# Second batch's pixels loaded uncast and added in rows on GpSimd, keys made two chunks at a time, and 17 instead of 14 GELU chunks on VectorE

## The chip, the cores and the metric

The kernel runs on one core of a Trainium2 chip. The metric is the device time of one execution in microseconds. Before the change it is 950.85 us (median of three runs, 950.6 to 951.17). The profile shown below is of one execution with a span of 949.0 us and a granted TensorE clock of 1.0.

## The reference

An attention over keys that are pooled from an image is followed by a feed-forward layer. Cut to what matters:

```
q: (4, 12288, 128)   kv: (4, 384, 32, 128)   w_sr: (128, 128)
w_in: (128, 2048)    w_out: (2048, 128)

kv_pool = mean over 4 x 4 pixels of kv            # (4, 96, 8, 128): 768 rows per batch
k = v   = kv_pool.reshape(4, 768, 128) @ w_sr
a       = softmax(q @ k^T / sqrt(128))
x       = (a @ v).reshape(49152, 128)
h       = x @ w_in
out     = (h * sigmoid(1.702 * h)) @ w_out        # float32
```

## The kernel before, in words

**Tiling.** The 49152 tokens are cut into 96 groups of 512 (`NG`), 24 per batch. The 768 keys of a batch are six chunks of 128 (`JC`), the 2048 hidden columns are sixteen chunks of 128 (`FCH`). The work goes in two rounds (`R`): attention of groups 0 to 47 (batches 0 and 1), then the feed-forward layer ("MoE") of these groups, then the same for groups 48 to 95. The outputs of attention of one round lie in the SBUF tile `x`, 12 slots of 2048 columns.

**Fill, activation, drain.** A fill multiplies into up to three PSUM banks (L340 for attention, L586 for MoE), one ScalarE activation takes the two or three banks at once (exponential at L342, GELU at L588) and writes into the ring `ag`, and a drain multiplies `ag` with the values (L353) or with `w_out` (L596). Two sets of three banks alternate, so that ScalarE works on one trio while TensorE fills the next. Banks 2, 5, 6 and 7 are for everything else (`acc`), later 6 and 7 alone. VectorE empties them: it divides the attention outputs (L376, L379), and transposes the MoE outputs into `o_sb` (L607), which SyncE stores.

**Chunks that ScalarE is spared.** Some exponentials and, in the second round, 14 GELU chunks (`lent`, one in every third group from 52 to 91) are computed by VectorE in short steps (`early_exp`, `lent_gelu`, L443 to L465) into the tile `aside`.

**The order.** The order of all instructions is written by the kernel itself: a planner at the end of the kernel walks over the fills, keeps a model of when TensorE, the banks and VectorE are free (`COST`, `COPY`, `RECIPROCAL`, in units of one 512-column matmul), and puts drains and extra jobs (`extras`) between the fills. Each engine works off its own queue in that order. `background(i)` is called when the first chunk of group `i` is about to be filled, and starts the loads, casts and stores that hang on this group.

**Keys of the second batch.** The first batch's pixels are loaded at the start. Those of batch 1 follow in `background(10)` and `background(12)`, three chunks each, by `load_chunk` (L130): GpSimd issues a DMA that casts from float32 to bf16, 128 partitions of 2048 columns. `pool_chunk` (L139 to L142) then sums on TensorE: sixteen matmuls with the 128 x 32 matrix `sum4`, four accumulated for each of four column groups, which add four pixels of a row and four rows. `key_and_value` (L161 to L164) multiplies the pooled chunk with `w_sr` for the keys and, transposed, for the values. From group 15 on one chunk's jobs are queued per group. The keys are needed at group 24.

**Queries.** They are cast to bf16 in DRAM by GpSimd's DMAs (`cast_q`, L209, at the groups in `CAST`), and brought back transposed by SyncE (`load_qT`, L215, at the groups in `TURN`). A block is four groups. `gate()` makes GpSimd wait for VectorE's place in the order: VectorE writes one element (L510), then GpSimd writes it (L511), and only then issues what follows.

**Outputs of attention** go to DRAM (`put_away`, L493) and come back transposed (`bring_back`, L499), both on SyncE.

Of the kernel before, what the change touches and what calls it, by code (L numbers as in the profile page):

```python
# [7 lines left out]
F32 = mybir.dt.float32  # L8
F32R = mybir.dt.float32r
I32 = mybir.dt.int32  # L10
BF = mybir.dt.bfloat16
AF = mybir.ActivationFunctionType
AX = mybir.AxisListType
ADD = mybir.AluOpType.add
# [10 lines left out]
def kernel(  # L25
    ctx, tc, q, kv, w_sr, moe_w_in, moe_w_out, out,
):
    nc = tc.nc
    B, N, C = q.shape
    _, H, W, _ = kv.shape  # L30
    r = 4
    Hp, Wp = H // r, W // r
    J = Hp * Wp
    JC = J // 128
    d_ff = moe_w_in.shape[1]
    FCH = d_ff // 128
    scale = 1.0 / (C ** 0.5)
    G = 512
    SG = 4 * G
    NG = B * N // G  # L40
    NS = NG // 4
    GB = NG // B
# [10 lines left out]
    kv_r = kv.rearrange("b (ch p) (a w) c -> b a ch p (w c)", p=128, a=2)  # L53
# [6 lines left out]
    XS = NS // R  # L60
# [7 lines left out]
    kvtmp = ctx.enter_context(tc.tile_pool(name="kvtmp", bufs=1))  # L68
# [3 lines left out]
    opool = ctx.enter_context(tc.tile_pool(name="op", bufs=3))  # L72
# [12 lines left out]
    def acc(key=None):  # L85

        nonlocal last_acc
        last_acc = next_acc()
        turns.append(last_acc)
        turns.remove(last_acc)  # L90
        if key:
            closes[last_acc] = key
        return banks[:, last_acc, :]

    def next_acc():
        return min((m for m in turns if m not in closes), key=lambda m: (max(free[m], now), turns.index(m)))
# [12 lines left out]
    x = xpool.tile([128, XS * SG], BF, name="x")  # L109

    def x_tile(s):
        return x[:, s % XS * SG:(s % XS + 1) * SG]
# [3 lines left out]
    HC = H // 128  # L116
    h = J // 2
    kv_tiles, kv_sums, pooled, pTs, kTs, vs = {}, {}, {}, {}, {}, {}

    def new_keys(b):  # L120
        kTs[b] = kvres.tile([128, J], BF, name="kT")

        vs[b] = kvres.tile([128, JC, C + 8], BF, name="v")
        nc.vector.memset(vs[b][:, :, C:C + 1], 1.0)

    def load_chunk(b, jc):

        a, ch = divmod(jc, HC)
        t = x_tile(XS - 1 - jc)
        nc.gpsimd.dma_start(out=t, in_=kv_r[b, a, ch])  # L130
        kv_tiles[b, jc] = t.rearrange("p (wp w1 c) -> p w1 wp c", w1=r, c=C)

    def pool_chunk(b, jc):
# [7 lines left out]
        pTs[b, jc] = kvtmp.tile([128, 128], BF, name="pTc", bufs=2)  # L141
        nc.vector.tensor_copy(pTs[b, jc], ps[:, 0:128])  # L142

    def key_chunk(b, jc):
        if jc == 0:
            new_keys(b)
        ps = acc()
        nc.tensor.matmul(ps[:, 0:128], w_sr_sb, pTs[b, jc], start=True, stop=True)
        nc.vector.tensor_copy(kTs[b][:, jc * 128:jc * 128 + 128], ps[:, 0:128])
# [5 lines left out]
        vs[b, jc] = True  # L155

    def key_and_value(b, jc):
        if (b, jc) == (1, 0):
            new_keys(b)
        ps = acc()  # L160
        nc.tensor.matmul(ps[:, 0:128], w_sr_sb, pTs[b, jc], start=True, stop=True)  # L161
        nc.tensor.matmul(ps[:, 128:256], pTs.pop((b, jc)), w_sr_sb, start=True, stop=True)
        nc.vector.tensor_copy(kTs[b][:, jc * 128:jc * 128 + 128], ps[:, 0:128])  # L163
        nc.vector.tensor_copy(vs[b][:, jc, 0:C], ps[:, 128:256])  # L164
        vs[b, jc] = True
# [41 lines left out]
    def cast_q(s):  # L207
        sl = slice(s * SG, (s + 1) * SG)
        nc.gpsimd.dma_start(out=q_bf[sl, :].rearrange("(p i) c -> p (i c)", p=128),  # L209
                            in_=q_flat[sl, :].rearrange("(p i) c -> p (i c)", p=128))  # L210

    def load_qT(s):
        qTs[s] = qpool.tile([128, 1, SG], BF, name="qT")
        nc.vector.memset(qTs[s][:, 0, 0:1], 0.0)
        nc.sync.dma_start_transpose(out=qTs[s], in_=q_bf[s * SG:(s + 1) * SG, :])  # L215
# [53 lines left out]
    for m in range(0, 128, 32):  # L269
        p = slice(m, m + 32)  # L270
# [3 lines left out]
    sum4 = cpool.tile([128, 32], BF)  # L274
# [3 lines left out]
    w_sr_sb = cpool.tile([128, C], BF)  # L278
# [40 lines left out]

    early = range(NG // R, NG // R + EARLY)  # L320
    rolling = [(i, JC - 1) for i in [*range(38, NG // R, 6), *range(57, 90, 6)]]
    lent = [(g, FCH - 1) for g in range(52, 94, 3)]
    aside = agpool.tile([128, K, 512], BF, name="aside")

    def weights(c):
# [112 lines left out]
    def lent_gelu(ps, out):  # L438
# [23 lines left out]
        for m in (0, 256):  # L462
            nc.vector.reciprocal(b[:, m:m + 256], a[:, m:m + 256])  # L463
            yield RECIPROCAL
        nc.vector.scalar_tensor_tensor(out, raw, -LN2 / 1.702, b, MUL, MUL)  # L465
# [21 lines left out]
    PART, FIRST = 24, 3  # L487

    def put_away(n, m):
        size = PART // 2 if n == 0 and m > FIRST else PART  # L490
        for o in range(m * PART, m * PART + PART, size):
            lo = n * XS * SG + o * T
            nc.sync.dma_start(out=x_bf[lo:lo + size * T, :].rearrange("(k p) c -> p k c", p=T),  # L493
                              in_=x[:, o * T:(o + size) * T].rearrange("p (k c) -> p k c", k=size))

    def bring_back(n, m):
        o = m * PART
        lo = n * XS * SG + o * T
        nc.sync.dma_start_transpose(out=x[:, o * T:(o + PART) * T].unsqueeze(1), in_=x_bf[lo:lo + PART * T, :])  # L499
# [6 lines left out]
    def gate():  # L506

        one = gate_tile[:, gates[0] % 8:gates[0] % 8 + 1]
        gates[0] += 1
        nc.vector.memset(one, 0.0)  # L510
        nc.gpsimd.memset(one, 0.0)  # L511

    TURN = {6: 3, 7: 4, 8: 5, 20: 6, 21: 7, 22: 8, 30: 9, 32: 10, 35: 11, 40: 12}
    CAST = {0: [5], 13: [6], 14: [7], 15: [8], 25: [9, 10], 26: [11, 12]}
    CAST_MOE = {20: 13, 21: 14, 22: 15, 23: 16, 33: 17, 34: 18, 35: 19, 36: 20, 37: 21, 38: 22, 39: 23}

    def background(i):

        first_round = i < GB * 2
        s = TURN.get(i, NS) if first_round else i // 4 + 3 if i % 4 == 0 else NS  # L520
        if s < NS:
            load_qT(s)
        if i in CAST:
            gate()
            for s in CAST[i]:
                cast_q(s)
        if i in (10, 12):
            gate()
            for jc in range(i % 10 * 3 // 2, i % 10 * 3 // 2 + 3):
                load_chunk(1, jc)  # L530
        if 0 <= i - 16 < JC:
            extras.append((key_and_value, 1, i - 16))
        if 0 <= i - 15 < JC:
            extras.append((pool_chunk, 1, i - 15))
        if i in (28, 33, 38):
            put_away(0, (i - 28) // 5)
        if i in (31, 36, 41):
            bring_back(0, (i - 31) // 5)
        if i == 27:
            gate()  # L540
            nc.gpsimd.dma_start(out=w_in_sb, in_=moe_w_in)
        if i == 28:
            gate()
            nc.gpsimd.dma_start(out=w_out_sb, in_=moe_w_out.rearrange("(o p) c -> p o c", p=128))

# [33 lines left out]
    extras = []  # L579
# [67 lines left out]
    for n in range(R):  # L647
        part = [c for c in chunks if c[0] // (NG // R) == n]
        while part:
            m = sizes.pop(0) if sizes else K  # L650
# [12 lines left out]
        while flat:  # L663
            m = K if len(flat) > sum(rest) else rest.pop(0)
# [25 lines left out]
    def jobs(p):  # L690

        nonlocal now
        for f, *args in first.get(p, ()):
            if f in COST:
                now = max(now, free[next_acc()])
            f(*args)
            if f in COST:
                now += COST[f][0]
                free[last_acc] = copied(f)

    def prepare(p):

        nonlocal now
        kind, part = seq[p]
        for i, jc in part:
            if (kind, i) not in begun:
                begun.add((kind, i))
                (background if kind == "a" else background_moe)(i)
            while kind == "a" and ((key_and_value, i // GB, jc) in extras or (transpose_q, i) in extras):
                f, *args = extras.pop(0)  # L710
                now = max(now, free[next_acc()]) + COST[f][0]
                f(*args)
                free[last_acc] = copied(f)
# [20 lines left out]


    FIXED, CHUNK, SWITCH, HANDOVER, EVACUATE = 0.295, 1.978, 6.0, 1.0, 4.5
    COST = {pool_chunk: (1.9, 2.6), key_chunk: (0.3, 2.4), value_chunk: (0.3, 2.4),
            transpose_q: (1.05, 4.2), early_fill: (1.0, 5.5), key_and_value: (0.55, 3.5),
            transpose_pooled: (0.9, 3.6), make_k: (0.8, 3.2), make_v: (0.8, 3.7)}
    COPY = {pool_chunk: 1.5, key_chunk: 1.5, value_chunk: 1.5, key_and_value: 2.8, transpose_q: 3.2}  # L740
    SMALL = 0.26
    RECIPROCAL = 10.5
    PAUSE = 4.0
    end, extra_at = [], 0.0
    source, dve = None, 0.0
# [2 lines left out]
    def on_dve(cost):  # L748
        nonlocal dve
        dve = max(dve, now + 1.0) + cost  # L750


    def copied(f):
        if f not in COPY:
            return now + COST[f][1]
        on_dve(COPY[f])
        return max(now + COST[f][1], dve)

# [28 lines left out]
    for n in range(len(seq)):  # L787
        fill(n + 2)
        jobs(n + 3)
        while True:  # L790
# [33 lines left out]
            kind, i, c = source[0]  # L824
# [11 lines left out]
            start = now if source is todo_early else max(now, end[needs] + HANDOVER)  # L836
            if first_of:
                start = max(start, bank)
# [44 lines left out]
```

The softmax here doesn't subtract the row's maximum and nothing guards it: scores larger than these inputs give would overflow.

## Time and profile before

| What | Value |
|---|---|
| time, median of 3 | 950.85 us |
| span of the profiled execution | 949.0 us |
| first exponential of ScalarE | 9.2 us |
| first attention phase, first GELU | to 142.3 us |
| first MoE phase | 142.3 to 487.7 us |
| second attention phase | 487.7 to 604.7 us |
| second MoE phase | 604.7 us to the end |
| VectorE busy from 604 to 937 us | 191.6 us of 333 |
| pixels of batch 1: loads issued | 39.0 to 46.4 us |
| pixels of batch 1: time to landing | 7.0 to 12.2 us |
| casts of query blocks 6, 7, 8: issued | 47.4, 49.1, 53.1 us |
| transposes of these blocks: start | 66.0, 68.9, 72.7 us |

How to read it: the page gives the busy time of each engine, the span in 40 slices, the DMA queues, the chain of work that ended last, and the costliest groups of instructions. A group's line names the source line, the engine, the operation, the tile written and read, and the shape; then the busy time, the mean of one in ns, and the idle time just before. A group of matmuls overlaps with itself, so its mean is longer than its pitch. The chain of waits can also be listed in order of time: start, length, and what led. The phases in the table are told apart by ScalarE's table loads [...].

### The profile page before, as it was taken

Reading aid. Unit: us, or ns where it says so; the run is one execution under the profiler, and the core shown is the slowest. Engines: PE = TensorE matmul, PEld = TensorE weight load, DVE = VectorE, ACT = ScalarE, POOL = GpSimd, SP = SyncE. Lnnn points to the kernel's source line nnn. Section 1 sums busy time; section 2 is a strip of 40 time slices with the busy share of each in tenths; the row PEclk is TensorE's granted clock in tenths of the full one; section 3 lists DMA queues with packets and bytes.
Section 4 is the critical chain, followed back from the end, with each engine's and each line's share of the span. In section 5 each row is a group of like instructions: output and inputs, shape, how many; then the busy total and the mean of one; then the engine's idle time right before and its main releaser. Section 6 shows DMA issues by size and latency. Waiting matters only on the chain.

```text
span 949.0 us, 15424 instructions
## 1 busy us (share of the span) xinstructions
PE 941.5 (99%) x6314; PEld 503.1 (53%) x6314; DVE 536.8 (57%) x1037; ACT 933.9 (98%) x708; POOL 67.0 (7%) x115
## 2 busy tenths in 40 slices
PE   8999999999999999999999999999999999999998
PEld 4677776444444444454446777754444444444444
DVE  5643553102477777778655765365666665566631
ACT  5999999999999999999999999999999999999998
POOL 4101001330000232000000000000000000000000
PEclk9999999999999999999999999999999999999999
DMA  9999922999867799865335583552222222222222
GB/s 182 203 181 193 214 57 42 157 127 170 162 132 113 116 147 125 123 103 78 65 55 112 133 160 77 134 122 35 44 34 45 34 46 34 45 33 45 34 45 45
DMA packets 372871, 94.93 MB, mean 100 GB/s; under 512 B 346736, under 2 KB 370416, under 8 KB 372464
## 3 DMA queue, kind: packets, MB, share of 16 engines
q1 hardware_dynamic: 343872, 61.31, 36.5%
q0 software_dynamic: 28656, 32.51, 22.6%
q8 instruction: 49, 0.80, 0.4%
q14 instruction: 22, 0.18, 0.1%
q10 hardware_dynamic: 272, 0.13, 0.0%
HBM read 52.49 MB, written 48.76 MB: 107 GB/s over the span
## 4 chain that ended last, share of the span: by engine, by line
ACT 88%; PE 9%; DMA 2%; issue 0%; DVE 0%; POOL 0%; POOLq 0%
ACT ag L588 71%; ACT ag L342 17%; PE banks L340 4%; PE banks L353 3%; DMA x<-in_kv_dram 1%; DMA qT<-q_bf 1%; PE banks L139 0%; PE banks L586 0%; PE banks L624 0%; ACT L588 0%; PE banks L596 0%; PE banks L233 0%; ACT L342 0%; DVE kT L163 0%; POOL x L222 0%
## 5 line engine op out<-in xcount | busy, mean ns | idle before, releaser
L588 ACT ACTIVATE ag<-banks 128x1536 bf16<-128x1536 f32 (+1 forms) x510 | 682.2, 1507 | 0.0
L586 PE MATMUL banks<-x,w_in_sb 128*128 128x512 bf16 x1522 | 411.7, 379 | 0.1
L596 PE MATMUL banks<-ag,w_out_sb 128*128 128x512 bf16 x1506 | 407.8, 379 | 0.0
L342 ACT ACTIVATE ag<-banks 128x1536 bf16<-128x1536 f32 (+2 forms) x192 | 245.8, 1439 | 3.7 <-PE banks L340 3.3
L596 PEld LDWEIGHTS <-w_out_sb 128*128 128x128 bf16 x1520 | 148.5, 98 | 178.0 <-issue 0.9
L586 PEld LDWEIGHTS <-w_in_sb 128*128 128x128 bf16 x1522 | 147.3, 98 | 170.4 <-issue 1.1
L607 DVE STREAM_TRANSPOSE o_sb<-banks 128x512 f32<-128x512 f32 x95 | 67.9, 715 | 210.7 <-PE banks L596 199.9
L353 PEld LDWEIGHTS <-ag 128*128 128x128 bf16 x2272 | 146.1, 98 | 46.4 <-issue 0.6
L353 PE MATMUL banks<-v,ag 128*128 128x129 bf16 x2272 | 163.7, 220 | 0.1
L340 PE MATMUL banks<-qT,kT 128*128 128x512 bf16 x544 | 148.7, 379 | 1.6 <-DVE kT L163 1.0
L432 DVE SCALAR_TENSOR_TENSOR ea<-ea,eb 128x512 f32<-128x512 f32 x128 | 87.8, 686 | 3.2
L376 DVE RECIPROCAL rec<-banks 128x3 f32<-128x3 f32 x124 | 22.2, 179 | 96.0 <-PE banks L353 96.0
L379 DVE TENSOR_TENSOR x<-banks,rec 128x384 bf16<-128x384 f32 x124 | 69.1, 557 | 4.3
L340 PEld LDWEIGHTS <-kT 128*128 128x128 bf16 x544 | 46.3, 98 | 26.6 <-DVE kT L163 1.7
L463 DVE RECIPROCAL eb<-ea 128x256 f32<-128x256 f32 x28 | 47.6, 1726 | 0.5
L173 POOL DMA_DIRECT2D kvs<-in_kv_dram x32 | 40.4, 1315 | 20.8 <-DMA kvs<-in_kv_dram 17.8
L421 DVE TENSOR_SCALAR ea<-banks 128x512 f32<-128x512 f32 x32 | 22.1, 692 | 32.6 <-PE banks L405 32.4
L456 DVE SCALAR_TENSOR_TENSOR ea<-ea,eb 128x512 f32<-128x512 f32 x56 | 38.3, 685 | 1.6
L511 POOL MEMSET gate_tile<- 1x1 f32 x37 | 3.9, 105 | 323.1 <-DVE gate_tile L510 323.1
L427 DVE SCALAR_TENSOR_TENSOR eb<-eb,ea 128x512 f32<-128x512 f32 x32 | 22.1, 690 | 0.9
L443 DVE TENSOR_SCALAR qT<-banks 128x512 f32<-128x512 f32 x14 | 9.7, 692 | 17.2 <-PE banks L399 16.9
L434 DVE SCALAR_TENSOR_TENSOR ag<-ea,ee 128x512 bf16<-128x512 f32 x24 | 16.5, 688 | 0.7
(84 smaller groups left out, 267.6 us busy)
## 6 DMA issues: line engine op xcount, KB each, us to landing
out_dram<-o_sb SPq DMA_DIRECT2D x380, 64.0 KB, 2.0
kvs<-in_kv_dram POOLq DMA_DIRECT2D x32, 384.0 KB, 6.5
q_bf<-in_q_dram POOLq DMA_DIRECT2D x21, 512.0 KB, 6.9
x_bf<-x SPq DMA_DIRECT2D x12, 768.0 KB, 5.8
x<-in_kv_dram POOLq DMA_DIRECT2D x12, 512.0 KB, 10.5
x_bf<-x SPq DMA_DIRECT2D x8, 384.0 KB, 4.5
x<-in_q_dram POOLq DMA_DIRECT2D x5, 256.0 KB, 15.2
w_in_sb<-in_moe_w_in_dram POOLq DMA_DIRECT2D x1, 512.0 KB, 9.6
```

The costliest lines, as they stand in the source:

```text
L173: nc.gpsimd.dma_start(out=kv_sums[b][:, i2], in_=kv_p[b, i, w, :, i2], **({"accum_op": ADD} if n else {}))
L340: nc.tensor.matmul(ps[:, k, :], kTs[i // GB][:, jc * 128:(jc + 1) * 128], rhs, start=True, stop=True)
L342: nc.scalar.activation(place([("a",) + c for c in chunks]), ps, AF.Exp, scale=scale)
L353: nc.tensor.matmul(av_of[u][:, k * (C + 1):(k + 1) * (C + 1)], weights(("a", i, jc))[:, o:o + T], vs[i // GB][:, jc, 0:C + 1], start=(jc = ...
L379: nc.vector.tensor_tensor(to, ps[:, :, 0:C], rec.unsqueeze(2).broadcast_to([128, TS, C]), MUL)
L432: nc.vector.scalar_tensor_tensor(a, a, COEFFS[k], b, ADD, MUL)
L456: nc.vector.scalar_tensor_tensor(a, a, COEFFS[k], b, ADD, MUL)
L463: nc.vector.reciprocal(b[:, m:m + 256], a[:, m:m + 256])
L586: nc.tensor.matmul(ps[:, k, :], w_in_sb[:, fc * 128:(fc + 1) * 128], x[:, g % (4 * XS) * G:(g % (4 * XS) + 1) * G], start=True, stop=True)
L588: nc.scalar.activation(place([("m",) + c for c in chunks]), ps, AF.Gelu_apprx_sigmoid)
L596: nc.tensor.matmul(o_of[g], w_out_sb[:, fc, :], weights(("m", g, fc)), start=(fc == 0), stop=(fc == FCH - 1))
L607: nc.vector.transpose(o_sb, o_of.pop(g))
```

## The change

It does four things.

1. The pixels of batch 1 come without a cast: SyncE loads each chunk as float32 (`load_pixels`), into three double slots of `x` that chunks 0 to 2 and then 3 to 5 use in turn. GpSimd adds the four pixels of a row group in three adds of 512 columns (`sum_pixels`), in place in float32 and last into bf16, in a borrowed `o_sb` buffer. The loads of chunks 3, 4 and 5 wait for the sums of 0, 1 and 2.
2. TensorE then has only four matmuls per chunk (`pool_sums`), taken two chunks at a time, and keys and values are made for two chunks at a time (`key_pair`). Pair jobs are queued at groups 15 and 16, 18 and 19, 21 and 22.
3. GpSimd's casts of queries stand between the sums in its queue, since both are issued in order of groups. Query block 9 is cast at group 16 and transposed at group 24, and blocks 10 to 12 and the MoE weights move a little.
4. `lent` takes the groups from 52 to 93 whose number ends in 2, 4, 7 or 9: 17 instead of 14. The planner's estimate of a reciprocal goes from 10.5 to 8.2.

Besides, one more `put_away` of the first round is split in halves. What it is for: the load of TensorE in the first attention phase, and that of ScalarE in the second MoE phase, is moved to GpSimd and VectorE.

```diff
+    def load_pixels(jc):
+        a, ch = divmod(jc, HC)
+        o = (XS - JC) * SG + jc % 3 * 2 * SG
+        t = x[:, o:o + 2 * SG].bitcast(F32)
+        if jc < 3:
+            nc.vector.memset(t[:, 0:1], 0.0)
+        nc.sync.dma_start(out=t, in_=kv_r[1, a, ch])
+        kv_tiles[1, jc] = t.rearrange("p (wp w1 c) -> p w1 wp c", w1=r, c=C)
+    def sum_pixels(jc):
+        t = kv_tiles.pop((1, jc))
+        if jc % 2 == 0:
+            held[jc // 2] = opool.tile([128, 512], F32, name="o_sb").bitcast(BF)
+        sums[jc] = held[jc // 2][:, jc % 2 * 512:jc % 2 * 512 + 512].rearrange("p (wp c) -> p wp c", c=C)
+        nc.gpsimd.tensor_tensor(t[:, 0], t[:, 0], t[:, 1], ADD)
+        nc.gpsimd.tensor_tensor(t[:, 2], t[:, 2], t[:, 3], ADD)
+        nc.gpsimd.tensor_tensor(sums[jc], t[:, 0], t[:, 2], ADD)
+    def pool_sums(b, jc):
+        ps = acc()
+        for k in range(2):
+            for wp in range(4):
+                o = k * 128 + 32 * wp
+                nc.tensor.matmul(ps[:, o:o + 32], sums[jc + k][:, wp, :], sum4, start=True, stop=True)
+        pTs[b, jc] = kvtmp.tile([128, 256], BF, name="pTp")
+        nc.vector.tensor_copy(pTs[b, jc], ps[:, 0:256])
+    def key_pair(b, jc):
+        if jc == 0:
+            new_keys(b)
+        ps = acc()
+        pT = pTs.pop((b, jc))
+        nc.tensor.matmul(ps[:, 0:256], w_sr_sb, pT, start=True, stop=True)
+        for k in range(2):
+            nc.tensor.matmul(ps[:, 256 + k * 128:384 + k * 128], pT[:, k * 128:(k + 1) * 128], w_sr_sb,
+                             start=True, stop=True)
+        nc.vector.tensor_copy(kTs[b][:, jc * 128:(jc + 2) * 128], ps[:, 0:256])
+        nc.vector.tensor_copy(vs[b][:, jc:jc + 2, 0:C], ps[:, 256:512].rearrange("p (k c) -> p k c", k=2))
...
-    lent = [(g, FCH - 1) for g in range(52, 94, 3)]
+    lent = [(g, FCH - 1) for g in range(52, 94) if g % 5 in (2, 4)]
...
-        size = PART // 2 if n == 0 and m > FIRST else PART
+        size = PART // 2 if n == 0 and m > 1 else PART
...
-    TURN = {6: 3, 7: 4, 8: 5, 20: 6, 21: 7, 22: 8, 30: 9, 32: 10, 35: 11, 40: 12}
-    CAST = {0: [5], 13: [6], 14: [7], 15: [8], 25: [9, 10], 26: [11, 12]}
+    TURN = {6: 3, 7: 4, 8: 5, 20: 6, 21: 7, 22: 8, 24: 9, 32: 10, 35: 11, 40: 12}
+    CAST = {0: [5], 13: [6], 14: [7], 15: [8], 16: [9], 25: [10, 11], 26: [12]}
...
-        if i in (10, 12):
-            gate()
-            for jc in range(i % 10 * 3 // 2, i % 10 * 3 // 2 + 3):
-                load_chunk(1, jc)
-        if 0 <= i - 16 < JC:
-            extras.append((key_and_value, 1, i - 16))
-        if 0 <= i - 15 < JC:
-            extras.append((pool_chunk, 1, i - 15))
+        if 10 <= i < 10 + JC:
+            if i > 10:
+                sum_pixels(i - 11)
+            for jc in range(3) if i == 10 else [i - 8] if i < 14 and i > 10 else []:
+                load_pixels(jc)
+        if i == 10 + JC:
+            sum_pixels(JC - 1)
+        if i in (15, 18, 21):
+            extras.append((pool_sums, 1, (i - 15) // 3 * 2))
+        if i in (16, 19, 22):
+            extras.append((key_pair, 1, (i - 16) // 3 * 2))
...
-        if i == 27:
+        if i == 26:
...
-        if i == 28:
+        if i == 27:
...
-    RECIPROCAL = 10.5
+    RECIPROCAL = 8.2
```

More of the change, by code (lines that the diff above doesn't have):

```diff
@@ L142, in pool_chunk @@
         nc.vector.tensor_copy(pTs[b, jc], ps[:, 0:128])
+    held, sums = {}, {}
+    def load_pixels(jc):
[33 more added lines that the diff above has]
+        nc.vector.tensor_copy(vs[b][:, jc:jc + 2, 0:C], ps[:, 256:512].rearrange("p (k c) -> p k c", k=2))
+        vs[b, jc] = vs[b, jc + 1] = True
     def key_chunk(b, jc):
@@ L157, in key_and_value @@
     def key_and_value(b, jc):
-        if (b, jc) == (1, 0):
-            new_keys(b)
         ps = acc()
@@ L708, in prepare @@
                 (background if kind == "a" else background_moe)(i)
-            while kind == "a" and ((key_and_value, i // GB, jc) in extras or (transpose_q, i) in extras):
+            while kind == "a" and ((key_pair, i // GB, jc // 2 * 2) in extras or (transpose_q, i) in extras):
                 f, *args = extras.pop(0)
@@ L736 @@
     FIXED, CHUNK, SWITCH, HANDOVER, EVACUATE = 0.295, 1.978, 6.0, 1.0, 4.5
-    COST = {pool_chunk: (1.9, 2.6), key_chunk: (0.3, 2.4), value_chunk: (0.3, 2.4),
+    COST = {pool_chunk: (1.9, 2.6), pool_sums: (1.1, 3.2), key_pair: (1.1, 5.0), key_chunk: (0.3, 2.4), value_chunk: (0.3, 2.4),
             transpose_q: (1.05, 4.2), early_fill: (1.0, 5.5), key_and_value: (0.55, 3.5),
             transpose_pooled: (0.9, 3.6), make_k: (0.8, 3.2), make_v: (0.8, 3.7)}
-    COPY = {pool_chunk: 1.5, key_chunk: 1.5, value_chunk: 1.5, key_and_value: 2.8, transpose_q: 3.2}
+    COPY = {pool_chunk: 1.5, pool_sums: 2.1, key_pair: 4.2, key_chunk: 1.5, value_chunk: 1.5, key_and_value: 2.8, transpose_q: 3.2}
     SMALL = 0.26
-    RECIPROCAL = 10.5
+    RECIPROCAL = 8.2
     PAUSE = 4.0
```

## The prediction

> **What bounds the kernel now.** I read the busy times first, then the shares of the chain of waits, then the chain in order of time, and last the single queues around the change.
>
> ```profile
> PE 941.5 (99%) x6314; PEld 503.1 (53%) x6314; DVE 536.8 (57%) x1037; ACT 933.9 (98%) x708; POOL 67.0 (7%) x115
> ...
> ACT 88%; PE 9%; DMA 2%; issue 0%; DVE 0%; POOL 0%; POOLq 0%
> ...
> L588 ACT ACTIVATE ag<-banks 128x1536 bf16<-128x1536 f32 (+1 forms) x510 | 682.2, 1507 | 0.0
> ...
> L463 DVE RECIPROCAL eb<-ea 128x256 f32<-128x256 f32 x28 | 47.6, 1726 | 0.5
> ```
>
> ScalarE is busy for 98% and owns 88% of the chain; PE's 99% is modelled. POOL is almost idle and DVE has 43% left: the change moves work to these two. The chain in order of time shows where each engine leads:
>
> ```profile
> 52.92 0.43 PE banks L139 x16
> ...
> 56.86 0.39 PE banks L139 x16
> ...
> 60.05 0.39 PE banks L139 x16
> 60.45 0.66 PE banks L340 x3
> ...
> 69.23 0.39 PE banks L139 x16
> ...
> 142.28 1.28 ACT L588
> 143.57 13.17 ACT ag L588 x10
> ...
> 487.68 1.28 ACT L342
> ```
>
> The first line dates the first pooling of the second batch, 0.39 us for each chunk on TensorE, in a stretch where PE pieces carry the chain. From 101 us on ScalarE carries it. Between the two table loads stand 256 activations of 1536 columns: (487.68 - 143.57) / 256 = 1.344 us for one. That is the price of three chunks on ScalarE.
>
> How much ScalarE loses in the first attention phase follows from a count: 28 activations of 1024 columns and 76 of 1536 from 13.11 us (the chain's third activation) to 142.28. The eight of 1024 columns at the end took 7.5 us, 0.94 each. 28 x 0.94 + 76 x 1.344 = 128.5 us, against 129.2. So relief of TensorE there can give back at most about 0.7 us.
>
> **The queues around the change**: SyncE's timeline, the pixel loads' time to landing, GpSimd's timeline with the cast that follows, a row of the stretches for the DMA share, and VectorE's largest group from 44 to 76 us.
>
> ```profile
> 35.13 4.75 SPq L215 DMA_TRANSPOSE qT<-q_bf  x2
> ...
> DMA to landing us min/median/max: 7.0/9.6/12.2
> ...
> 47.17 0.09 POOL L511 MEMSET gate_tile<- 1x1 f32 x1 [0.23 <-DVE gate_tile L510]
> 47.41 0.51 POOL L209 DMA_DIRECT2D q_bf<-in_q_dram  x1
> ...
> 46.00:48.00 2.00, 2.00 (x28) 1.53 (x25) 0.75 (x4) 2.00 (x3) 1.53 (x4) 1.00 1.08 213
> ...
> L379 DVE TENSOR_TENSOR x<-banks,rec 128x384 bf16<-128x384 f32 x13 | 7.2, 557 | 0.4
> ```
>
> SyncE is through with its transposes at 39.9 us. The first pixel load, issued at 39.0, landed 7.0 us later, at 46.0; the DMA share (column before the last) is 1.08, so the engines are full. A gate with its cast holds GpSimd for 47.92 - 47.17 = 0.75 us.
>
> [...] No add ran on GpSimd here; the kindred VectorE row is 685 ns for 512 columns (L456). [...]
>
> **The change part by part.**
> 1. **Three more GELU chunks on VectorE** (14 to 17). ScalarE's second MoE phase has one activation of 1536 columns fewer: -1.34 us, on the chain. VectorE pays per chunk, from its rows: 0.692 + 3 x 0.427 + 0.692 + 0.420 + 4 x 0.685 + 0.688 + 0.424 + 2 x 1.726 + 0.665 = 11.1 us. Three are 33 us. From 604 to 937 us VectorE was busy 191.6 of 333 us, so it goes to 225, 68%. Behind a reciprocal of 1.73 us queues the stream transpose that frees an output bank (0.715 us, waited 107 us in total in that stretch for TensorE); a group lasts 16/3 x 1.344 = 7.2 us, so a delay of 1.7 us hides. The new RECIPROCAL constant (8.2 planning units) only shifts the order. Cost: nothing on the chain.
> 2. **Pooling matmuls**: 96 of 32 columns become 24. At 0.39 / 16 = 0.024 us each, TensorE saves 72 x 0.024 = 1.8 us. The key and value matmuls keep their columns (256 + 2 x 128 per pair). ScalarE can take at most the 0.7 us worked out above; I take 0.3. VectorE copies 9 times instead of 18, about 1 us less, off the path.
> 3. **GpSimd's sums.** Each chunk needs three adds of 512 columns. [...] I take 1.17[...], so 3.5 us a chunk. Six chunks in a row, with a gate and cast after the second, third, fourth and fifth. Start: the loads go out on SyncE when it is free, 39.9 us; I take landing at 46.0 as now, 44.5 to 47 as ends. Then sums 0 and 1 are ready at 46.0 + 7.0 = 53.0; sums 2 and 3 at 53.0 + 2 x (0.75 + 3.5) = 61.5; sums 4 and 5 at 70.0. Chunks 3 to 5 reload a slot when its sum is done (49.5, 53.0, 57.2), and have 8 us or more before their own sum begins, so they hide. TensorE's pair jobs stand, by the order of the built program, after the same fills as chunk 0 (52.9), one trio of fills after chunk 2 (60.45 + 0.66 = 61.1), and as chunk 5 (69.2). So TensorE waits 0.1, then is 0.4 and 0.8 us late in total. Behind the waiting matmul queue all fills and drains, and ScalarE waits for the fills. Three fills take 0.65 us of a pitch of 1.34, so they are 0.7 us ahead: 0.8 - 0.7 = 0.1 us reach ScalarE.
> 4. **Casts of queries behind the sums.** Cast 6 leaves at about 53.8 us, 8 at 62.3, 9 at 66.5. The transposes that need 6 to 8 ran at 66.0, 68.9 and 72.7 us; the cast of 8 left at 53.06 and the DMA was full, after the change it has 10 us. Hidden. Query block 9 moves from group 30 to 24; now TensorE waited 0.2 us for such a block at 100.5. At most 0.2 us gained, counted in the 0.3.
> 5. **put_away in halves, weights one group earlier, the memsets as waits**: hidden by the DMA queue's lead of tens of us before 142 us.
>
> Sum: 950.85 - 1.34 - 0.3 + 0.1 = 949.3 us.
>
> **The rivals.**
> *GpSimd is late (slower).* [...] ready at 54.1, 63.7, 73.2, lateness 1.2, 2.6, 4.0; 4.0 - 0.7 = 3.3 us reach ScalarE: 950.85 - 1.64 + 3.3 = 952.5. Landing a microsecond later makes it 953.5[...]. For the rival speaks that the lead is so small: 0.2 us on an add costs over 3 us.
> *TensorE's relief is worth all it can be.* If the sums are in time [...] and all 0.7 us plus small waits return: 950.85 - 1.34 - 0.7 - 0.3 = 948.5. For it: PE pieces lead the chain until 93 us. Against it: ScalarE idles only 0.11 us from 50 to 75.
> *VectorE becomes the bound in the second MoE phase.* Each late output bank would stall a drain; then the three chunks give nothing: 950.6. Against it: 32% of idle time remains.
>
> **How the numbers follow.** Forecast 0.50, GpSimd late 0.26, full relief 0.19, VectorE 0.05. The border of faster, 0.2%, is 948.95; a third of the forecast's case (spread half a microsecond) and nearly all of full relief lie below it: 0.35. The border of slower is 952.75: most of the first rival with later landing or loading, 0.24. Same: 0.41. The range reaches from 948.0 (below full relief) to 953.5 (late sums with late landing)[...].
>
> **What would show it.** Right: one L588 activation fewer at the same pitch; [...] the pair matmuls waiting for GpSimd by less than 1 us; no ScalarE idle from 50 to 75 us. Wrong: TensorE waiting for o_sb's sums by several us; a gap before GpSimd's first add; stream transposes of the second MoE phase delayed until ScalarE idles.

## The result, and the profile after

The changed kernel takes 954.62 us (median of six runs, 953.13 to 955.75) against 950.8 us; the ratio of the means is 1.0035, with a 95% interval of 1.0022 to 1.0048. It is slower by 0.35%, where 949.3 us was forecast. The profiled execution has a span of 951.4 us at a granted clock of 1.0, 2.4 us above that of before.

The page of the changed kernel: busy times, shares of the chain, and ScalarE's two groups (GELU at L634, exponential at L385). The last line is the exponential in the kernel before.

```profile
PE 939.2 (99%) x6239; PEld 501.2 (53%) x6239; DVE 567.4 (60%) x1075; ACT 933.2 (98%) x707; POOL 85.6 (9%) x126
...
PE 48%; ACT 47%; DMA 3%; POOL 2%; issue 0%; DVE 0%; SPq 0%; POOLq 0%
...
L634 ACT ACTIVATE ag<-banks 128x1536 bf16<-128x1536 f32 (+1 forms) x509 | 680.9, 1502 | 0.1
...
L385 ACT ACTIVATE ag<-banks 128x1536 bf16<-128x1536 f32 (+2 forms) x192 | 246.2, 1432 | 7.0 <-PE banks L383 6.7
```

```profile
L342 ACT ACTIVATE ag<-banks 128x1536 bf16<-128x1536 f32 (+2 forms) x192 | 245.8, 1439 | 3.7 <-PE banks L340 3.3
```

The work moved as planned: TensorE and ScalarE have less, VectorE and GpSimd more. But ScalarE's exponentials now wait 7.0 us in place of 3.7, and in the chain TensorE, DMA and GpSimd stand where ScalarE led. GpSimd's timeline (start, length, line, tiles, idle before) tells why:

```profile
45.80 1.26 POOL L162 TENSOR_TENSOR x<-x 128x512 f32<-128x512 f32 x1 [26.80 <-DMA x<-in_kv_dram]
...
49.60 1.27 POOL L162 TENSOR_TENSOR x<-x 128x512 f32<-128x512 f32 x1
...
53.38 0.09 POOL L554 MEMSET gate_tile<- 1x1 f32 x1
53.42 0.52 POOL L252 DMA_DIRECT2D q_bf<-in_q_dram  x1
53.95 1.28 POOL L162 TENSOR_TENSOR x<-x 128x512 f32<-128x512 f32 x1
...
65.24 1.27 POOL L164 TENSOR_TENSOR o_sb<-x 128x512 bf16<-128x512 f32 x1
...
69.36 1.27 POOL L162 TENSOR_TENSOR x<-x 128x512 f32<-128x512 f32 x1 [2.36 <-DMA x<-in_kv_dram]
```

A chunk's three adds take 49.60 - 45.80 = 3.80 us, a gate and a cast from 53.38 to 53.95, 0.57 us. Before the last chunk GpSimd stands 2.36 us for its load. The chain from 48 to 76 us (start, length, what led) goes through this load to TensorE:

```profile
57.83 11.46 DMA x<-in_kv_dram
...
71.92 1.27 POOL o_sb L164
73.20 0.05 issue
73.24 0.27 PE banks L172 x4
```

The load was issued at 57.83 us, when its slot was free, and landed 11.46 us later. TensorE reached the last pair in time and waited; so did ScalarE behind it. The waits of the two engines from 50 to 76 us (total, times, longest):

```profile
PE banks L172 <- POOL o_sb L164: 3.1, 2, 2.8
PE banks L172 <- POOL gate_tile L554: 0.6, 1, 0.6
...
ACT ag L385 <- PE banks L383: 3.4, 3, 2.9
```

ScalarE's table loads, one of 1.28 us at each change between exponential and GELU, date the loss. The following table is read from ScalarE's timeline, also for four of the runs described below: the second MoE phase starts at its table load, "last" is the start of the last activation, and the tail runs from there to the end of the span (us).

| kernel | first GELU load | second MoE load | last | span | second MoE | tail |
|---|---|---|---|---|---|---|
| before | 142.28 | 604.70 | 942.96 | 949.0 | 338.3 | 6.0 |
| changed | 146.27 | 608.78 | 945.74 | 951.4 | 337.0 | 5.6 |
| gelu_alone | 142.60 | 605.02 | 941.94 | 949.5 | 336.9 | 7.6 |
| pooling_alone | 146.53 | 609.05 | 947.40 | 952.7 | 338.4 | 5.3 |
| cast_loads | 141.90 | 604.41 | 941.36 | 947.3 | 337.0 | 6.0 |
| cast_loads_14 | 142.07 | 604.80 | 943.15 | 948.9 | 338.4 | 5.8 |

The first GELU comes 4.0 us later; the second MoE phase with its tail is 1.7 us shorter.

### The profile page after: what moved, and what is told of

Its sections match the earlier page's. It is cut to its first block, busy times and chain, and to the rows that moved or that the text cites. A ratio compares the mean times of both kernels' runs of the same rounds, so it can differ in the third digit from the quotient of the medians.

```text
span 951.4 us, 15343 instructions
## 1 busy us (share of the span) xinstructions
PE 939.2 (99%) x6239; PEld 501.2 (53%) x6239; DVE 567.4 (60%) x1075; ACT 933.2 (98%) x707; POOL 85.6 (9%) x126
## 4 chain that ended last, share of the span: by engine, by line
PE 48%; ACT 47%; DMA 3%; POOL 2%; issue 0%; DVE 0%; SPq 0%; POOLq 0%
ACT ag L634 35%; PE banks L632 18%; PE banks L642 17%; ACT ag L385 12%; PE banks L396 6%; PE banks L383 5%; DMA x<-in_kv_dram 3%; PE banks L448 1%; POOL o_sb L164 1%; POOL x L162 1%; POOL x L163 1%; PE banks L670 0%; PE banks L139 0%; PE banks L276 0%; ACT L634 0%
## 5 line engine op out<-in xcount | busy, mean ns | idle before, releaser
L634 ACT ACTIVATE ag<-banks 128x1536 bf16<-128x1536 f32 (+1 forms) x509 | 680.9, 1502 | 0.1
L385 ACT ACTIVATE ag<-banks 128x1536 bf16<-128x1536 f32 (+2 forms) x192 | 246.2, 1432 | 7.0 <-PE banks L383 6.7
L475 DVE SCALAR_TENSOR_TENSOR ea<-ea,eb 128x512 f32<-128x512 f32 x128 | 87.5, 684 | 3.8 <-DVE ea L475 0.6
L506 DVE RECIPROCAL eb<-ea 128x256 f32<-128x256 f32 x34 | 57.8, 1724 | 0.5
L499 DVE SCALAR_TENSOR_TENSOR ea<-ea,eb 128x512 f32<-128x512 f32 x68 | 46.6, 686 | 2.0
L486 DVE TENSOR_SCALAR qT<-banks 128x512 f32<-128x512 f32 x17 | 11.8, 691 | 22.9 <-PE banks L442 22.6
```

The costliest lines, as they stand in the source:

```text
L385: nc.scalar.activation(place([("a",) + c for c in chunks]), ps, AF.Exp, scale=scale)
L475: nc.vector.scalar_tensor_tensor(a, a, COEFFS[k], b, ADD, MUL)
L499: nc.vector.scalar_tensor_tensor(a, a, COEFFS[k], b, ADD, MUL)
L634: nc.scalar.activation(place([("m",) + c for c in chunks]), ps, AF.Gelu_apprx_sigmoid)
```

## The experiments

"Before" is the kernel before, measured beside each run; every ratio is one of means. The changed kernel again:

> The changed kernel once more, beside the others on one chip. From its first profile: first GELU table load at 146.3 us, GpSimd waits 2.4 us for the load of pixel chunk 5, ScalarE idles 2.9 us once at 71.6 us, span 951 us. Time 953 to 955 us.

Measured: 954.6 us against 951.21, ratio 1.0032 (1.0019 to 1.0044); first GELU load at 146.07 us. The slowdown repeats.

### Is it the reload, or GpSimd's adds?

```diff
-        nc.sync.dma_start(out=t, in_=kv_r[1, a, ch])
+        if jc < 3:
+            nc.sync.dma_start(out=t, in_=kv_r[1, a, ch])
```

> Leaves out the loads of pixel chunks 3, 4 and 5: GpSimd adds what lies in the three slots a second time, with the same adds and casts. Theory 1 (the reloaded slot is late: chunk 5's load lands 11.5 us after its issue): the wait of 2.4 us goes, the sums are ready at 53.4, 62.2 and 70.9 us, and ScalarE loses about 1.7 us between 50 and 75 us instead of 4.2; first GELU table load at about 143.9, time 2.4 us below the changed kernel, about 951. Rival (the adds alone are too slow: 1.27 us each where 1.17 was taken): first GELU stays near 146 us and the time near 953.5.

Measured: 950.8 us, ratio 0.9997 (0.9988 to 1.0005), first GELU load at 143.78 us. TensorE's waits from 45 to 140 us:

```profile
PE banks L173 <- POOL o_sb L165: 1.5, 3, 0.6
```

The 2.8 us wait is gone, three small ones of at most 0.6 us stay. Theory 1 holds in size: the first GELU comes 146.07 - 143.78 = 2.3 us earlier than in the changed kernel beside it, where 2.4 was expected. The time falls by more, 3.8 us; the part on the clock, at the end, takes that up. The rest of the lateness, 143.78 - 142.28 = 1.5 us, has the size of the three small waits: it is GpSimd's own work.

### Why did the load take 11.5 us?

```diff
-    CAST = {0: [5], 13: [6], 14: [7], 15: [8], 16: [9], 25: [10, 11], 26: [12]}
+    CAST = {0: [5], 25: [10, 11], 26: [12]}
...
```

> Leaves out the casts of query blocks 6 to 9 and reads block 5 in their place; loads and sums as in the changed kernel. Theory 1a (the casts slow the loads: their packets are 32 KB beside 8 KB of the loads, and 2.4 us beside 0.31): chunks 3, 4 and 5 all land within 6 us of their issue, the sums are ready at 53.4, 61.0 and 68.6 us, ScalarE loses under 0.5 us from 50 to 75 us, first GELU at about 142.5 us, time about 949.3. Rival 1b (a load that waits for its slot is late by itself): chunk 5 still lands 8 us or more after its issue, and GpSimd still waits for it.

Measured: 949.39 us, ratio 0.9981 (0.9974 to 0.9989), first GELU load at 142.81 us. The load of chunk 5 in the changed kernel, and then without the casts (time to landing; one load, so the three numbers agree):

```profile
DMA to landing us min/median/max: 11.5/11.5/11.5
```

```profile
DMA to landing us min/median/max: 4.7/4.7/4.7
```

So the load by itself takes 4.7 us; the query casts beside it cost 6.8 us more, and rival 1b falls. GpSimd is also spared its four casts here, so the time of this run is not the price of the load alone. One wait of TensorE for sums, 0.7 us, stays.

The second question was whether bytes or packets decide. The casts were cut into shorter runs:

```diff
-        nc.gpsimd.dma_start(out=q_bf[sl, :].rearrange("(p i) c -> p (i c)", p=128),
-                            in_=q_flat[sl, :].rearrange("(p i) c -> p (i c)", p=128))
+        rows = "(a p i) c -> p a (i c)" if 6 <= s <= 9 else "(a p i) c -> (a p) (i c)"
+        nc.gpsimd.dma_start(out=q_bf[sl, :].rearrange(rows, p=128, a=2 if 6 <= s <= 9 else 1),
+                            in_=q_flat[sl, :].rearrange(rows, p=128, a=2 if 6 <= s <= 9 else 1))
```

> The changed kernel with the casts of query blocks 6 to 9 written as 128 x 2 runs of 1024 columns, not 16 runs of 16384, the same bytes. Theory (long cast packets take the DMA engines from the loads[...]): chunk 5 lands within 7 us of its issue, GpSimd no longer waits for it, the sums come at 53.4, 62.3 and 71 us, ScalarE loses 1.7 us from 50 to 75 us; first GELU at about 143.9, time about 950.8 as in the run without second loads. Rival (the sum of bytes counts, not the packets): chunk 5 lands more than 9 us after its issue and the time stays at 953 to 955.

Measured: 952.02 us, ratio 1.001 (1.0003 to 1.0016), first GELU load at 144.47 us. Chunk 5 landed after 7.8 us, between the theory's 7 and the rival's 9, and GpSimd waited for no load but the first. The DMA queues from 52 to 70 us (packets, MB, share of 16 engines; q0 has the casts, q1 the loads), changed kernel first, then short runs:

```profile
DMA packets 511, 4.96 MB, mean 276 GB/s; under 512 B 96, under 2 KB 96, under 8 KB 96
q0 software_dynamic: 111, 2.06, 58.3%
q1 hardware_dynamic: 397, 2.86, 44.1%
```

```profile
q1 hardware_dynamic: 890, 2.89, 56.0%
q0 software_dynamic: 816, 1.57, 49.4%
```

18 us of 16 engines are 288 us. In the changed kernel 48 packets of each queue carry only 4 bytes; the other 63 of q0 are the casts' packets of 32 KB, so one takes 0.583 x 288 / 63 = 2.7 us on average (2.43 at the least). With short runs q0 has 768 packets of 2 KB, 0.494 x 288 / 768 = 0.19 us each. A load's packet of 8 KB takes 0.441 x 288 / 349 = 0.36 us. In the trace of the changed kernel a cast of a block is 16 packets, and no packet of a load starts from 57.1 to 58.5, from 61.6 to 63.0 and from 65.9 to 68.5 us, while those of the casts of blocks 6, 7 and 8 run. Chunk 5's load meets some 1.9 us of the first (from 57.83 to about 59.7 us) and, with its last packets, 2.5 us of each of the others: 6.9 us as an estimate, for 6.8 lost.

The same bytes in short packets gave back 3.7 of the 6.8 us. So here about half of the loss goes with the length of the packets, and the rest stays with the same bytes in short ones. The time fell less than expected (950.8), and the first GELU came 0.6 us later than expected: TensorE still waited 1.1 us for sums and 1.0 us for a gate.

### The parts by themselves

```diff
-    lent = [(g, FCH - 1) for g in range(52, 94, 3)]
+    lent = [(g, FCH - 1) for g in range(52, 94) if g % 5 in (2, 4)]
...
-    RECIPROCAL = 10.5
+    RECIPROCAL = 8.2
```

> The kernel before with part 4 alone: 17 GELU chunks on VectorE, reciprocal estimate 8.2. Theory: one ScalarE activation fewer, 1.34 to 1.7 us off the second MoE phase: 949.1 to 949.5 us. Rival (VectorE becomes the bound, or the new order costs elsewhere): 950.3 us or more.

Measured: 951.16 us, ratio 1.0 (0.9991 to 1.0008). The rival's number. But the second MoE phase did shrink on ScalarE, from 338.3 to 336.9 us. The tail took it back, 7.6 us in place of 6.0. The end of the chain, before and then with GELU alone:

```profile
942.49 0.43 PE banks L586 x2
942.92 2.69 PE banks L624 x48
...
945.64 0.51 DVE o_sb L632 x2
```

```profile
941.90 0.45 PE banks L596 x2
942.34 0.02 issue
942.36 0.73 DVE o_sb L607
943.09 0.04 issue
943.13 3.02 PE banks L624 x51
```

When ScalarE is done earlier, TensorE isn't: it still drains the last group but one, VectorE has to transpose that bank, and only then come the 51 matmuls of the last group. TensorE's own backlog sets the end. When the last activation starts, all 64 matmuls of the last group are still to come, against 48 in the kernel before and 40 in the changed kernel, at 2.69 / 48 = 0.056 us each. The opposite half, parts 1 to 3 with 14 GELU chunks:

> The changed kernel with 14 GELU chunks and the old reciprocal estimate: parts 1 to 3 alone. Theory (TensorE is a second bound: GELU alone gave nothing because 51 drains stood behind the last activation, so the two parts pay only together): ScalarE's second MoE phase is one activation longer than in the changed kernel, 1.3 us; time 1.3 us above it, about 955.9. Rival (TensorE's relief pays by itself at the end): the time is within 0.5 us of the changed kernel.

Measured: 955.94 us, ratio 1.0049 (1.0034 to 1.0064), 1.3 us above the changed kernel's 954.6, as the theory had it. The first GELU load stands at 146.53 us, so the whole loss comes from parts 1 to 3.

### Later pair jobs

```diff
-        if i in (15, 18, 21):
-            extras.append((pool_sums, 1, (i - 15) // 3 * 2))
-        if i in (16, 19, 22):
-            extras.append((key_pair, 1, (i - 16) // 3 * 2))
+        if i in (16, 19, 22):
+            extras.append((pool_sums, 1, (i - 16) // 3 * 2))
+        if i in (17, 20, 23):
+            extras.append((key_pair, 1, (i - 17) // 3 * 2))
```

> The changed kernel with the pair jobs queued one group later (16 and 17, 19 and 20, 22 and 23). Theory (TensorE reaches the sums before GpSimd has them, and ScalarE loses that lateness whole): demand moves 2.7 us to 55.6, 63.8 and 71.9 us, the sums come at 53.4, 62.2 and 73.2, so only the last is late, by 1.3 us; first GELU table load at 143.7, time 2.6 us below the changed kernel, about 951. Rival (the last keys then come too late for group 24 at about 76 us): the wait moves to the first fill of group 24 and the first GELU stays past 145 us.

Measured: 954.66 us, 951.4 to 962.9 in 13 runs, ratio 1.0046 (1.0025 to 1.0068). In the profiled execution (962.9 us, the slowest) TensorE waited 2.4 us for the last sums and 4.8 us for query block 6, whose transpose landed after 19.3 us. Stretches of it: PE, PEld, DVE, ACT and POOL busy, clock, DMA share, GB/s.

```profile
70.00:75.00 5.00, 2.64 (x34) 1.99 (x33) 1.28 (x5) 2.97 (x3) 3.72 (x3) 0.93 1.46 74
75.00:80.00 5.00, 4.78 (x41) 3.48 (x41) 2.03 (x6) 3.14 (x3) 0.00 (x0) 0.73 1.10 85
80.00:85.00 5.00, 0.61 (x6) 0.22 (x4) 0.06 (x1) 1.10 (x1) 0.00 (x0) 0.95 1.26 46
85.00:90.00 5.00, 4.33 (x28) 3.29 (x29) 0.79 (x3) 2.81 (x2) 0.00 (x0) 0.50 1.17 219
90.00:95.00 5.00, 5.00 (x49) 3.47 (x49) 1.69 (x9) 3.81 (x4) 2.06 (x7) 0.87 1.07 237
```

Behind each idle stretch the granted clock was lower: 0.73 on average from 75 to 80 us, 0.50 from 85 to 90. TensorE was slow there: in the chain twelve drains took 1.30 us from 86.03 and again from 88.61 us, and 0.68 from 95.48. The missing clock of these rows adds up to (0.07 + 0.27) x 5 = 1.7 us from 70 to 80 us and (0.05 + 0.50 + 0.13) x 5 = 3.4 us from 80 to 95. The rival was right that the wait moves to group 24, though for another cause than late keys: late queries.

> Short cast runs and pair jobs one group later together. Theory: sums at 53.4, 62.3 and 71 us stand before the demand at 55.6, 63.8 and 71.9; ScalarE loses under 0.4 us from 50 to 75 us, first GELU at about 142.3 us, time about 949.0, below both kernels. Rival (something else holds ScalarE in this stretch): first GELU past 143 us, time 950 or more.

Measured: 955.63 us, 950.11 to 961.83 in 20 runs, ratio 1.0042 (1.0026 to 1.0057). All 20 missed the theory's 949.0 us. The profiled execution (span 949.6 us, first GELU at 143.90 us) shows TensorE waiting 0.4 us for sums and 1.4 us for a query block, and no fall of the clock (1.00 from 60 to 100 us). The others come in steps of the mean clock: spans of 948.1 to 950.8 us at a mean clock of 1.0, 952.3 to 953.7 at 0.998, 954.5 to 957.2 at 0.996, 960.1 at 0.995. Missing clock of 1.7 us, as in jobs_later from 70 to 80 us, makes a step of 1.7 / 952 = 0.002 (see the part on the clock below). What TensorE waited for in them is open; the execution profiled in jobs_later is the nearest evidence.

```diff
-    TURN = {6: 3, 7: 4, 8: 5, 20: 6, 21: 7, 22: 8, 24: 9, 32: 10, 35: 11, 40: 12}
-    CAST = {0: [5], 13: [6], 14: [7], 15: [8], 16: [9], 25: [10, 11], 26: [12]}
+    TURN = {6: 3, 7: 4, 8: 5, 20: 6, 21: 7, 22: 8, 30: 9, 32: 10, 35: 11, 40: 12}
+    CAST = {0: [5], 13: [6], 14: [7], 15: [8], 25: [9, 10], 26: [11, 12]}
...
```

> Pair jobs one group later as in the run jobs_later, and query block 9 cast at group 25 and transposed at group 30 again, as in the kernel before. Theory (with later jobs the wait moved to query block 6, whose transpose took 19 us beside the casts of blocks 8 and 9): the transpose of block 6 lands by 77 us, the only loss is about 1 us at the last pair, spread of the times under 2 us, time about 951. Rival (cast 9 is not what starves it): the transpose still takes over 12 us in the profile and the times spread from 951 to 960 as before.

Measured: 955.48 us, 954.51 to 956.83 in four runs, ratio 1.0048 (1.0034 to 1.0062). Block 6 landed 6.5 us after its issue, at 73.0, as the theory had it, and the spread is 2.3 us where under 2 was expected. But the time, about 951 us, was missed; TensorE's waits from 30 to 145 us:

```profile
PE banks L172 <- POOL o_sb L164: 2.6, 1, 2.6
PE banks L448 <- DMA qT<-q_bf: 2.5, 1, 2.5
```

Chunk 5 took 12.3 us to land here, and query block 9, back at its old place, now came too late for the early exponential at 103 us. The earlier cast of block 9 in the change had a use.

### Only the loads put back

```diff
-        o = (XS - JC) * SG + jc % 3 * 2 * SG
-        t = x[:, o:o + 2 * SG].bitcast(F32)
-        if jc < 3:
-            nc.vector.memset(t[:, 0:1], 0.0)
-        nc.sync.dma_start(out=t, in_=kv_r[1, a, ch])
+        t = x_tile(XS - 1 - jc)
+        nc.gpsimd.dma_start(out=t, in_=kv_r[1, a, ch])
...
-            for jc in range(3) if i == 10 else [i - 8] if i < 14 and i > 10 else []:
-                load_pixels(jc)
+            if i == 10:
+                gate()
+                for jc in range(JC):
+                    load_pixels(jc)
```

> The changed kernel with the pixels loaded as before, by six casting DMAs of GpSimd into six slots at group 10, and GpSimd's adds reading bf16; jobs and query casts as in the changed kernel. Theory (a slot that is reloaded behind a sum and beside the query casts is what comes late): all six chunks land by 59 us, GpSimd never waits for a load after the first, sums at about 53.6, 62.3 and 71 us, ScalarE loses about 1.7 us from 50 to 75 us, time about 951. Rival (GpSimd's own work is what is late, and bf16 adds are no faster): the same loss as in the changed kernel, 953 us or more.

Measured: 949.44 us, 949.02 to 950.55 in 20 runs, ratio 0.9982 (0.9976 to 0.9989): 1.7 us better than the kernel before (951.11 beside it) and better than the changed one. GpSimd's groups from 44 to 75 us:

```profile
L159 POOL TENSOR_TENSOR x<-x 128x512 bf16<-128x512 bf16 x6 | 7.0, 1161 | 3.4 <-DMA x<-in_kv_dram 3.4
L161 POOL TENSOR_TENSOR o_sb<-x 128x512 bf16<-128x512 bf16 x6 | 6.9, 1154 | 0.5
```

The only wait for a load is that before the first add, and the adds are shorter too, 1.16 us in bf16 beside 1.27. The last sum was ready at 68.6 us, before TensorE's 69.2, so not 1.7 us were lost as expected, but none: from 45 to 140 us neither TensorE nor ScalarE shows a wait, and the first GELU stands at 141.90 us. The run changes two things, the reload and the speed of the adds; what each is worth is not told apart.

With later jobs as well, and block 9 at its old place:

> Pixels loaded as before into six slots, pair jobs one group later, query block 9 cast and transposed as in the kernel before; GpSimd's sums, pair jobs and 17 GELU chunks kept. Theory: no wait for a load, the sums stand before the demand (53.6, 62.3, 71 against 55.6, 63.8, 71.9), the DMA queues are as in the kernel before; ScalarE loses under 0.4 us from 50 to 80 us, first GELU at about 142.2 us and the second MoE phase is 1.3 us shorter: 949.0 to 949.5 us, below both kernels. Rival (GpSimd in this stretch costs something else, the casts behind its sums above all): 950.5 us or more.

Measured: 953.99 us, ratio 1.0033 (1.0021 to 1.0045). The theory was wrong on the queries. Just after 100 us TensorE waited 2.2 us for block 9, and then ran slowly:

```profile
PE banks L445 <- DMA qT<-q_bf: 2.2, 1, 2.2
```

```profile
100.00:105.00 5.00, 3.08 (x17) 1.99 (x18) 1.12 (x2) 1.52 (x2) 0.00 (x0) 0.69 0.99 217
```

The clock averaged 0.69 over these 5 us, and ScalarE stood for 3.7 us of 95 to 110 us after a recorded wait of 2.2. And cast_loads with 14 GELU chunks:

> The run cast_loads with 14 GELU chunks and the old reciprocal estimate: GpSimd's sums and the pair jobs alone, without a late load. Theory (TensorE and ScalarE bind together, so that 17 GELU chunks alone gave nothing and pay 1.3 us only beside TensorE's relief): first GELU at 141.9 us as in cast_loads, the second MoE phase 1.3 us longer on ScalarE, time about 950.6, 0.5 us below the kernel before. Rival (the relief alone carries the gain): 949.5 us or less.

Measured: 950.8 us, ratio 0.9997 (0.9989 to 1.0006). With no late load, parts 1 to 3 alone change nothing that can be measured. 17 GELU chunks alone change nothing either. Both together save 951.11 - 949.44 = 1.7 us: in the table, with TensorE relieved, the second MoE phase is 1.4 us shorter and the tail only 0.2 us longer (6.0 against 5.8); without relief the tail ate it.

How a saving before 75 us reaches the end shows in the drains that TensorE has started. At the start of the 51st activation of the first MoE phase they are 129 in the changed kernel and in cast_loads, 120 in the kernel before; at the phase's last activation 732 and 724. The planner, which has less to place in the attention phase, sets the drains earlier, and the lead of some eight drains stays. At 0.43 us for two in the chain, eight are 1.7 us, about the 1.8 us that the pooling matmuls gave.

## Why the prediction was wrong, point by point

**What failed is step 3**, GpSimd's sums. Its forecast for the last pair was 70.0 us, the measured time 73.2. The terms:

- "hide", said of the reload of chunks 3 to 5: chunk 5 took 11.5 us where about 9 stood between its issue and its sum, and GpSimd waited 2.4 us. The step priced the load by the distance alone and not beside the casts which the same change puts next to it; even the landing times quoted from the kernel before, 7.0 to 12.2 us with a median of 9.6, did not all fit into "8 us or more". This is the largest term, shown by leaving out the loads and by leaving out the casts.
- an add of 1.17 us measured 1.27: 18 x 0.1 = +1.8 us. The 1.17 was the author's estimate; the kernel before has no add on GpSimd that shows it.
- the gate with its cast, 0.75 us, measured 0.57: 4 x 0.18 = -0.7 us. The landing at 46.0 was 45.8: -0.2 us. Together 70.0 + 2.4 + 1.8 - 0.7 - 0.2 = 73.3.
- "0.7 us ahead": there is no such slack. TensorE was 73.2 - 69.2 = 4.0 us late and the first GELU came 4.0 us late. Whatever the fills run ahead, the fixed order behind them found no time to catch up.

**Step 4** was right for the casts themselves and wrong in what it left out: what they do to the loads. With later jobs their effect reached query block 6 as well.

**Step 1** held on ScalarE: 338.3 - 337.0 = 1.3 us for a price of 1.34, and VectorE didn't become the bound. Its claim that this lies on the end's path by itself did not hold: alone it gave 0. **Step 2** held in its phase (cast_loads: 0.4 us for 0.3), but missed the worth of the 1.8 us of TensorE: carried along as earlier drains, they are what lets the GELU chunks pay at the end. cast_loads, where the sums do come in time, runs in 949.44 us, near the 949.3 forecast. Part of that is another way of loading and faster adds, so it doesn't prove the forecast's sum.

**The rival "GpSimd is late"** had the sign and the chain of causes right, and put it down to the price of the adds. That its 73.2 us for the last sums is the measured time is luck: it took a slower add than the 1.27 us measured, an estimate that no trace of before shows, and no wait for a load. It was held to be half as likely as the forecast, though its own text said that 0.2 us on an add costs over 3 us: a chain with so little room was no place for a small probability.

**The clock, and what stays open.** The profile accounts for 2.4 us, the medians differ by 3.8. The eleven executions of the changed kernel are of two kinds: four at a mean clock of 1.0 have spans of 950.9 to 951.4 us, seven at 0.998 have 952.6 to 954.0. The seven are 1.8 us longer on average, 953.0 against 951.2. Missing clock of 1.7 us, as in jobs_later from 70 to 80 us, makes a mean of 1 - 1.7 / 952 = 0.998. The 27 executions of no_second_loads and no_casts, without the long wait, are all at 0.999 or 1.0.

When the clock falls is not shown. Behind waits of TensorE of 2.4 and 4.8 us in jobs_later it was 0.73 and 0.50 over 5 us, and in the 5 us with the wait of 2.2 us in cast_loads_later it was 0.69. Yet in the profiled execution of the changed kernel the wait was 2.8 us, and the clock was 1.00 from 70 to 80 us; in that of later_cast9_back the waits were 2.6 and 2.5 us, at a mean clock of 1.0. So the length of a wait alone doesn't tell these cases apart. No execution of the changed kernel with a fall was profiled, so that its fall lies at this wait is not shown directly.

## What to carry to other kernels

A buffer that is loaded again behind a computation needs the time of its load beside everything that is in the DMA queues then: count the packets of the others and their length, not only the bytes (here 7.8 us to landing beside packets of 2 KB, 11.5 beside 32 KB). Where two engines are full, as here, taking work off one can be worth nothing until the other is relieved too; look at the work left on each behind the other's last instruction. When a static order feeds an engine from one that has no slack, lateness can pass through whole, as the 4.0 us did here. And a wait of TensorE can cost more than itself through the clock: behind the 2.4 us in jobs_later it was 0.73 over 5 us, behind the 2.8 us in the changed kernel's profiled execution 1.00.

## What the runs showed of the hardware

A query cast between two DRAM tensors in the changed kernel went out in 16 packets of 32 KB, of 2.43 us at the least and 2.7 on average, and beside such casts a load of 1 MB took 11.5 us, in place of 4.7 without them. Beside casts in packets of 2 KB it took 7.8 us. The granted clock was 0.73 over the 5 us behind a wait of TensorE of 2.4 us and 0.50 behind one of 4.8 us (jobs_later), 0.69 over the 5 us with one of 2.2 us (cast_loads_later), and 1.00 behind one of 2.8 us (changed kernel). The transpose of a query block, 4.1 us from issue to landing in the kernel before (66.03 to 70.11), took 10.2 us beside casts in the changed kernel and 19.3 us in one execution of jobs_later. Adds of 512 float32 columns on GpSimd took 1.27 us each and followed each other within a chunk every 1.22 to 1.35 us; in bf16 they took 1.16 us and followed every 1.11 to 1.24. The first add started 0.2 us after its data had landed (45.6 and 45.8 us). A table load of ScalarE took 1.28 us.
